# Retention attention and a top-2 mixture of experts: three more early pieces, from a fourth weight buffer laid over the attention output

## The chip, the cores and the metric

The kernel runs on one core of one Trainium2 chip. The metric is the device time of one execution in microseconds, the median of several runs. A profile of one further execution gives where each engine was busy or idle. The engines are called PE (matrix products), ACT, DVE and POOL (element-wise work; POOL also issues the indirect transfers) and SP (issues most of the other transfers).

## The reference

Attention with a decay over 8 batches, 8 heads, 576 positions and a head size of 64 gives 4608 tokens of 512 values. A router picks the two best of 8 experts for each token, and each expert is two products of 512 x 1024 and 1024 x 512 with a relu between them.

```
scores = q @ k^T / sqrt(64)
x      = (scores * Dmat) @ v                      # Dmat: gamma[h] ** (row - column), 0 above the diagonal
x      = x.transpose(0, 2, 1, 3).reshape(4608, 512)
noisy  = x @ w_gate + log1p(exp(x @ w_noise)) * noise
top2   = the two largest of noisy in each row; weights = softmax over these two
for e in 0..7:
    rows = tokens that have e among their two
    out[rows] += weight * (relu(x[rows] @ w1[e]) @ w2[e])
```

All inputs and the output are 32-bit floats in device memory. The weights of one expert are 4 MB.

## The kernel before, in words

**Attention and routing.** The 8 batches are worked in four pairs (`bp` 0 to 3). The attention output of a pair is kept turned in an `xT` buffer (two buffers, used in turn: 128 partitions x 4608 values of bf16 each). `route(bp)` computes the router for the pair from it, gives every (token, expert) choice a place in that expert's list, makes the table `xi{bp}` of which token stands at which place, turns the rows back (L1096) and stores them with their weights to `xd` in device memory (L1105, issued by SP).

**Pieces.** The list of an expert has 1216 places, cut in 9 pieces of 128 and one of 64. Choices where the expert is the lower-numbered of a token's two come first (`FIRST` says how many places they have). Places fill in the order of the tokens, so the first places of a list are known before the last pair is routed. `CLOSE` says, for each of the first three routings and each expert, up to which place the list is held to be closed after it. Pieces below that mark are run early; if too few tokens have come, the places up to the mark stay empty and later tokens go behind it.

**Early tiles.** `tiles()` makes early tiles of up to two pieces. `fetch` gathers their rows from `xd` (L1232, POOL), turns them on PE (L1254). `up` is the first product (L1314) with a relu on ACT (L1323) or DVE (L1325), `down` the second (L1404). `finish` scales the result by the token's weight (L1457 on ACT, L1459 on DVE) and scatters it to the output (L1469, POOL). Before the change there are 9 early tiles: 6 pieces of expert 0, 5 of expert 1, 4 of expert 2.

**Wide tiles.** After the last routing the other pieces run in tiles of up to four (512 columns). `wide` is their first product (L1340); the second product of the tile before is woven into it (L1404; L1423 for the piece of 64). Their rows are gathered up to three tiles ahead and turned by DMA (L1244, issued by SP), except those of expert 3, which PE turns (L1254). Gathers are spaced by `PACE`.

**Weights.** There are three weight buffers of 2 MB in bf16 (`W`). Experts 0 to 2 come early by converting transfers that POOL issues (L1145, L1149). The weights of a later expert come in 8 parts of 512 KB: SP loads a part as 32-bit floats into a buffer `big` (L1169, L1172; at most 4 `big` buffers for this), and ACT or DVE casts it into `W` (L445, L447). `weights(e + 3)` is called at the last tile of expert e, so expert 3 takes the buffer of expert 0, expert 4 that of expert 1, and so on. `SPREAD` says after how many steps (one step is one of the 8 column groups of a wide tile) the next part is due: 0 for expert 3, 3 for 4 and 5, 4 for 6 and 7.

**Order.** Every operation is recorded with a cost, its readers and writers and a priority. The planner `Plan.run` then sets the order on each engine before anything is issued: it simulates the engines and takes, again and again, the operation that can start earliest, and among equals the one of the smaller priority number. Buffers are granted in the order of recording within each class and use. Each engine, SP included, then works its list strictly in that order, and waits on the chip are those that the data and buffers need. A tile `i` has the priority 100 + 4 i. A table `ORDER` adds an offset for each kind of operation, by the range that the priority is in: the last two of its six columns are for 60 to below 136, and for 136 and above.

Of the kernel before, what the change touches and what calls it, by code (L numbers as in the profile page):

```python
# [10 lines left out]
BF16 = mybir.dt.bfloat16  # L11
I32 = mybir.dt.int32
# [5 lines left out]
P = 128  # L18
N = 4608
NCOL = N // P  # L20
E = 8
F = 1024
DM = 512
KD = DM // P
KF = F // P
HPE = 10
CAP = 1216
NH = E * HPE
# [2 lines left out]
SPREAD = (0, 0, 0, 0, 3, 3, 4, 4)  # L31
PACE = 2.343
AHEAD = (2, 3)
CLOSE = ((256, 0, 0, 0, 0, 0, 0, 0), (512, 384, 384, 0, 0, 0, 0, 0), (768, 640, 512, 0, 0, 0, 0, 0))
PLW = 8
XW = DM // 2 + PLW
ORDER = {
# [154 lines left out]
C9 = 9  # L192
# [211 lines left out]
class Kernel:  # L404
    def __init__(self, tc, ctx, src, gates, noise, w1, w2, out, xd):
        self.tc, self.nc = tc, tc.nc
        self.src, self.gates, self.noise, self.w1, self.w2, self.out = src, gates, noise, w1, w2, out
        self.xd = xd
        nc = self.nc
        self.pl = pl = Plan()  # L410
        self.cp = ctx.enter_context(tc.tile_pool(name="fix", bufs=1))
        self.ps = ctx.enter_context(tc.tile_pool(name="ps", bufs=1, space=bass.MemoryType.PSUM))
        mk = lambda n, k, sh, dt: [(self.cp.tile(sh, dt, name=f"{n}{i}"), None) for i in range(k)]
        bs = [self.cp.tile([P, 2, 1024], F32, name=f"big{i}") for i in range(5)]
        pl.cls("big", [(x[:, i, :], x) for x in bs for i in range(2)], exp=4, xt=3, rt=1)
        pl.cls("half", mk("half", 21, [P, 512], F32), cs=9, exp=15, xt=3, tl=6, rt=1)
        pl.cls("tb", mk("tb", 5, [P, 2, 4, P], BF16))
        pl.cls("xT", mk("xT", 2, [P, KD, C9, P], BF16))
        xs = [self.cp.tile([P, 2, XW], F32, name=f"xg{i}") for i in range(12)]
        pl.cls("xg", [(x[:, i, :], x) for x in xs for i in range(2)], exp=14, rt=10)  # L420
        pl.zone["xg", "exp"], pl.zone["xg", "rt"] = (10, 24), (0, 10)
        ws = [self.cp.tile([P, KD * F + KF * DM], BF16, name=f"W{i}") for i in range(3)]
        pl.cls("W", [(x, None) for x in ws])
        part = lambda x, i, n: x[:, 2 * i * n:2 * i * n + 2 * n].bitcast(F32)
        pl.cls("wkv", [(part(x, i, 2048), None) for x in ws[1:] for i in range(2)])
        pl.cls("wq", [(part(ws[0], i, 1024), None) for i in range(4)])
        pl.cls("ps", [(self.ps.tile([P, 512], F32, name=f"ps{i}"), None) for i in range(8)], exp=4, xt=2, rt=2, tl=2, rw=2, att=7)
        pl.cls("pay", mk("pl", 2, [P, 3], F32))
        self.fixed = {}
        pl.warm = self.warm  # L430
        self.xdk, self.outk = pl.fix(), {}
        self.writes, self.reads, self.firsts = [], [], {e: [] for e in range(E)}
# [493 lines left out]
    def route(self, bp, prio):  # L926
        pl, nc, f = self.pl, self.nc, self.fix
# [3 lines left out]
        xT = self.xT.pop(bp)  # L931
# [28 lines left out]
        m1, w2, rs, d2, x = (f(n, [P, C]) for n in ("max1", "wb", "rs", "d2", "low1"))  # L960
# [50 lines left out]
        pr = self.psum("rt")  # L1011
# [56 lines left out]
                                 start=(c == 0), stop=(c == 2 * C - 1), skip_group_check=True)  # L1068
        pl.op("PE", 1.3, table, r=[olo, oh], w=[(pT, 0)], prio=prio, late=0, at="route40")
        L = f("L", [P, NH])  # L1070
        xi = f(f"xi{bp}", [P, HPE * 3 if bp < 3 else NH], I32)
        nx = xi.t.shape[1]
        if bp == 0:
            o("DVE", 0.25, lambda e: V.tensor_copy(xi.t, pT.t[:, :nx]), [(pT, 0)], [xi], at="route41")
# [13 lines left out]
        for g in ((0, 2), (2, 2), (4, 2), (6, 2), (8, 1)):  # L1088
            c, n = g
            p, xr = self.psum("rw"), pl.buf("xg", "rt", 2)  # L1090

            def rows(e, c=c, n=n, p=p):
                o_ = p.t.bitcast(BF16).rearrange("p (c d) -> p c d", c=2)
                for k in range(n):
                    for di in range(KD):
                        nc.tensor.transpose(o_[:, k, di * P:(di + 1) * P], xT.t[:, di, c + k, :], ident.t)  # L1096
            b = c // 4
            rd = [(xT, (hq, b, e)) for hq in range(2) for e in range(2)] if b < 2 else [(xT, (2, 0)), (xT, (2, 1))]
            o("PE", 0.31 * n, rows, rd + [ident], [p], at="route47")
            o({"ACT": 0.17 + 0.43 * n, "DVE": 0.15 + 0.28 * n}, 0, lambda e, n=n, p=p, xr=xr: self.copy(  # L1100
                e, xr.t.bitcast(BF16)[:, :n, :DM], p.t.bitcast(BF16).rearrange("p (c d) -> p c d", c=2)[:, :n]), [p], [(xr, 0)], prio=prio + 1, at="route48")
            o({"POOL": 0.3, "DVE": 0.2}, 0, lambda e, c=c, n=n, xr=xr: self.eng(e).tensor_copy(
                xr.t[:, :n, DM // 2:], pay.t[:, c:c + n, :]), [pay], [(xr, 1)], at="route49")
            row = 1 + (c0 + c) * P
            pl.op("SP", 0.55, lambda e, n=n, xr=xr, row=row: nc.sync.dma_start(  # L1105
                out=self.xd[row:row + n * P, :].rearrange("(c p) w -> p c w", p=P), in_=xr.t[:, :n]),
                r=[xr], w=[(self.xdk, (bp // 2, bp, c))], prio=prio, dma=n * 0.4, at="route50")

# [27 lines left out]

    def weights(self, e, prio, cast_dma, after=()):
        pl, nc = self.pl, self.nc
        w = self.W[e] = pl.buf("W", "exp")
        if cast_dma:  # L1140
            for k in range(0, 8, 2):
                def go(_, k=k):
                    o = w.t[:, k * F:(k + 2) * F]
                    if k < KD:
                        nc.gpsimd.dma_start(out=o.rearrange("p (do f) -> p do f", do=2),  # L1145
                                            in_=self.w1[e, k * P:(k + 2) * P, :].rearrange("(do di) f -> di do f", di=P))
                    else:
                        fo = 2 * (k - KD)
                        nc.gpsimd.dma_start(out=o.rearrange("p (fo d) -> p fo d", fo=4),  # L1149
                                            in_=self.w2[e, fo * P:(fo + 4) * P, :].rearrange("(fo fi) d -> fi fo d", fi=P))  # L1150
                self.wdma.append(pl.op("POOL", 0.85, go, w=[(w, k), (w, k + 1)], prio=prio, dma=2.9,
                                       after=list(after) + self.wdma[-2:-1], at="weights1"))
            return
        for k in range(8):
            self.parts.append((self.step + SPREAD[e] * k, e, k))
        self.due(prio, after)
# [353 lines left out]
    def record(self):  # L1510
        pl = self.pl
# [9 lines left out]
        for u in range(NU + 1):  # L1521
            bp = u // 4
# [31 lines left out]
        for e, u in enumerate(WAIT):  # L1554
            raw = (("wkv", "att"), ("wq", "att"))[e == 0]
            self.weights(e, (40, 14.6, 14.7)[e], True, landed(u) + [o for b in pl.fifo[raw] for o in b.ops])

        fetched = 0
        for i, t in enumerate(ts[:ne]):
# [12 lines left out]
        for i in range(ne, len(ts) + 1):  # L1572
# [4 lines left out]
            if i < len(ts):  # L1577
# [5 lines left out]
                            self.before(i, ts[i], s, pr - 4)  # L1583
                if i == last[E - 2]:
                    self.before(i, ts[i], [self.size(j) for j in ts[i][1]].index(CAP % P), pr)
                if i == last[e] and e + 3 < E:
                    self.weights(e + 3, pr, False, begun)
                begun = [self.wide(i, ts[i], pr, prev)]
            else:
                e, po, hT = ts[-1][0], self.t[i - 1]["po"], self.t[i - 1]["hT"]  # L1590
# [141 lines left out]
```

## Time and profile before

| | |
|---|---|
| timed runs | 414.92, 413.98, 415.88 us; median 414.92 |
| span of the profiled execution, first to last instruction | 423.6 us (no other time of that execution is given) |
| PE busy | 379.1 us (89%) |
| POOL, ACT, DVE busy | 277.5, 271.2, 147.8 us |
| data moved by DMA | 98.06 MB, 231 GB/s over the span |
| last routing's table is built (L1067) | 161.5 to 162.4 us |
| first wide tile begins (L1340) | 191.2 us |
| expert 3's weight loads are issued | 188.5 to 208.7 us |

The span is cut below into stretches by these points: attention with routing and early tiles, early tiles alone, wide tiles. In rows of a timeline the first number is the start in us from the beginning of the span, the second the duration, and in brackets stands how long the engine was idle before it and what ended that. "issue" means that the profile shows nothing the engine waited for.

### The profile page before, as it was taken

What the parts mean: (1) busy time and instruction counts of PE and PEld (TensorE: products, weight loads), DVE (VectorE), ACT (ScalarE), POOL (GpSimd) and SP (SyncE); (2) the same over time, 40 slices, a digit from 0 to 9 for tenths busy, and PEclk for the clock granted to TensorE, in tenths of its full rate; (3) what the DMA queues carried; (4) which work ended last, traced back from release to release, by engine and by line L of the source; (5) the groups of instructions that cost most, each with busy time, mean ns of one, the idle gap of its engine ahead of it and who ended that gap; (6) DMA issues with size and microseconds to landing.
All of it is one profiled execution on the core that took longest, in us unless ns stands there. A gap on an engine that the chain in (4) does not pass through costs nothing.

```text
span 423.6 us, 10900 instructions
## 1 busy us (share of the span) xinstructions
PE 379.1 (89%) x4252; PEld 233.2 (55%) x4286; DVE 147.8 (35%) x415; ACT 271.2 (64%) x466; POOL 277.5 (66%) x345
## 2 busy tenths in 40 slices
PE   6898869777998997879999999999999896999993
PEld 2567657666676775645565544544544442454452
DVE  7357797896498595000313220200010000000002
ACT  3489978896887763545675796576676371655550
POOL 8577766872799465555476766777656672628554
PEclk9899998999999999999999999999999997999999
DMA  8999999999989994669899999999999999959775
GB/s 227 290 305 272 320 300 295 289 248 256 322 200 236 248 254 150 142 174 307 240 279 367 271 234 272 277 219 274 235 213 146 266 164 223 196 79 128 128 92 123
DMA packets 106184, 98.06 MB, mean 231 GB/s; under 512 B 40975, under 2 KB 83472, under 8 KB 106130
## 3 DMA queue, kind: packets, MB, share of 16 engines
q1 hardware_dynamic: 85858, 60.92, 56.2%
q0 software_dynamic: 17584, 36.24, 42.6%
q8 instruction: 34, 0.56, 0.6%
q10 hardware_dynamic: 2688, 0.18, 0.4%
q14 instruction: 20, 0.16, 0.1%
HBM read 73.11 MB, written 26.10 MB: 234 GB/s over the span
## 4 chain that ended last, share of the span: by engine, by line
PE 49%; DMA 20%; issue 9%; DVE 9%; POOL 6%; ACT 4%; ACTq 0%; POOLq 0%; SPq 0%; another core or an unknown queue 0%; DVEq 0%
PE ps L1404 17%; PE ps L1340 14%; DMA xg<-xd,xi 7%; PE ps L1314 6%; POOL out_dram L1469 5%; DMA big<-xg 3%; DMA out_dram<-half,im 3%; DMA out_dram<-half,xg 2%; DMA W<-in_moe_w_dram 2%; PE ps L794 2%; DVE half L769 2%; PE ps L829 2%; ACT half L445 1%; DMA W<-in_q_dram 1%; PE ps L453 1%
## 5 line engine op out<-in xcount | busy, mean ns | idle before, releaser
L1404 PE MATMUL ps<-W,half 128*128 128x512 bf16 x543 | 181.0, 382 | 6.2 <-ACT half L1323 4.7
L1340 PE MATMUL ps<-big,W 128*128 128x512 bf16 (+4 forms) x631 | 179.7, 331 | 6.6 <-issue 4.6
L1323 ACT ACTIVATE half<-ps 128x512 bf16<-128x512 f32 (+5 forms) x181 | 89.0, 508 | 73.3 <-PE ps L1340 47.5
L1232 POOL DMA_INDIRECT xg<-xd,xi x76 | 78.3, 1031 | 68.1 <-issue 18.3
L1469 POOL DMA_INDIRECT out_dram<-half,xg x71 | 90.7, 1278 | 33.0 <-issue 13.9
L1340 PEld LDWEIGHTS <-W 128*128 128x128 bf16 x640 | 62.9, 98 | 54.7 <-issue 8.5
L1404 PEld LDWEIGHTS <-half 128*128 128x128 bf16 x568 | 55.0, 98 | 68.5 <-ACT half L1323 7.0
L445 ACT ACTIVATE W<-big 128x1024 bf16<-128x1024 f32 x37 | 38.7, 1059 | 19.8 <-DMA big<-in_moe_w_dram 19.8
L1457 ACT ACTIVATE half<-ps,xg 128x512 f32<-128x512 f32 (+1 forms) x61 | 41.4, 679 | 13.1 <-PE ps L1404 12.0
L445 ACT ACTIVATE half<-ps 128x1024 bf16<-128x1024 bf16 (+1 forms) x40 | 37.6, 962 | 12.2 <-remote 3.6
L769 DVE TENSOR_TENSOR half<-ps,mask 128x512 bf16<-128x512 f32 x64 | 40.0, 682 | 14.1 <-PE ps L761 10.7
L1325 DVE TENSOR_SCALAR half<-ps 128x192 bf16<-128x192 f32 (+3 forms) x15 | 7.5, 500 | 78.0 <-PE ps L1340 19.8
L1314 PE MATMUL ps<-half,W 128*128 128x256 bf16 (+1 forms) x288 | 30.3, 255 | 1.9 <-issue 1.7
L1314 PEld LDWEIGHTS <-W 128*128 128x128 bf16 x288 | 23.7, 98 | 5.9 <-issue 2.3
L1455 DVE SCALAR_TENSOR_TENSOR half<-ps,xg,half 64x256 f32<-64x256 f32 (+2 forms) x7 | 3.6, 521 | 62.3 <-PE ps L1423 39.5
L445 ACT ACTIVATE tb<-ps 64x512 bf16<-64x512 f32 x32 | 18.9, 590 | 8.5 <-PE ps L794 6.2
L453 PE MATMUL ps<-mask,ident__61 128*128 128x512 bf16 x66 | 20.2, 439 | 3.7 <-DVE hpf L513 3.7
L1459 DVE TENSOR_SCALAR half<-ps,xg 64x256 f32<-64x256 f32 (+1 forms) x14 | 8.3, 596 | 42.9 <-PE ps L1423 21.0
L445 ACT ACTIVATE xT<-ps 128x512 bf16<-128x512 f32 (+1 forms) x32 | 16.2, 552 | 3.1 <-PE ps L879 1.8
L794 PE MATMUL ps<-half,half 64*64 64x64 bf16 (+2 forms) x512 | 16.8, 210 | 1.6 <-issue 0.9
L445 ACT ACTIVATE xg<-ps 128x1024 bf16<-128x1024 bf16 (+1 forms) x19 | 17.0, 939 | 1.8 <-PE ps L1096 1.1
L761 PE MATMUL ps<-half,half 64*64 64x128 bf16 x512 | 11.7, 218 | 7.1 <-ACT half L445 4.1
(196 smaller groups left out, 434.8 us busy)
## 6 DMA issues: line engine op xcount, KB each, us to landing
big<-in_moe_w_dram SPq DMA_DIRECT2D x40, 512.0 KB
W<-in_moe_w_dram POOLq DMA_DIRECT2D x12, 512.0 KB
xd<-xg SPq DMA_DIRECT2D x16, 264.0 KB
W<-in_q_dram SPq DMA_DIRECT2D x16, 256.0 KB
big<-in_k_dram SPq DMA_DIRECT2D x8, 512.0 KB
big<-in_v_dram SPq DMA_DIRECT2D x8, 512.0 KB
big<-in_q_dram SPq DMA_DIRECT2D x16, 256.0 KB
W<-in_k_dram SPq DMA_DIRECT2D x6, 512.0 KB
```

The costliest lines, as they stand in the source:

```text
L445: self.nc.scalar.activation(out, in_, Act.Copy)
L453: self.nc.tensor.matmul(b.t, lhsT=ident, rhs=mask.rearrange("p r x -> p (r x)").unsqueeze(1).to_broadcast([P, 2, 2 * P]), start=True, stop ...
L761: nc.tensor.matmul(o[h][e * HD:(e + 1) * HD, c, r], lhsT=kt[s, hp, c, r, e, :], rhs=qt[s, hp, :, 16 * j:16 * j + 16], start=(c == 0 and r ...
L769: nc.vector.tensor_tensor(S.t.bitcast(BF16).rearrange("p (h c x) -> p h c x", h=2, c=2)[:, h], p[h].t.rearrange("p (c x) -> p c x", c=2), ...
L794: nc.tensor.matmul(o[h * HD:(h + 1) * HD, hp, n, :], lhsT=kk[:k, r, c, y], rhs=vv[:k, r, c, y].unsqueeze(1).to_broadcast([k, n.stop - n.st ...
L1232: ins = nc.gpsimd.indirect_dma_start(out=x.t[:n, :], out_offset=None, in_=self.xd[:rows, :], in_offset=IOff(ap=xi.t[:n, h:h + 1], axis=0), ...
L1314: nc.tensor.matmul(pv()[:, f2, :], lhsT=w.t[:, o:o + P], rhs=xv()[:, di, :n], start=(di == 0), stop=(di == KD - 1))
L1323: self.nc.scalar.activation(o, i, Act.Relu)
L1340: self.mm = nc.tensor.matmul(p.t[:, :n], lhsT=w.t[:, o:o + P], rhs=xv()[:, di, :n], start=(di == 0), stop=(di == KD - 1))
L1404: self.mm = self.nc.tensor.matmul(po.t, lhsT=hv[:, c:c + P], rhs=self.W[e].t[:, o:o + DM], start=(f == 0), stop=(f == KF - 1))
L1457: nc.scalar.activation(y.t[q, c], x, Act.Copy, scale=g()[q])
L1469: ins = nc.gpsimd.indirect_dma_start(out=self.out[:, :], out_offset=IOff(ap=ix()[q2], axis=0), in_=y.t[q2, :], in_offset=None, bounds_chec ...
```

## The change

`CLOSE` gets 384 for expert 3 after the third routing, so pieces 0 to 2 of expert 3 become two early tiles (two pieces, and one) behind the nine; its wide pieces are now 7, in tiles of 4 and 3. Their priorities are 136 and 140, and all wide tiles' numbers rise by 8. The table `xi2` is widened from 30 to 40 columns to hold expert 3.

The two `xT` buffers become halves of one tile, and a fourth weight buffer `W4` (8192 of the 9216 values of a partition) is laid over them. Expert 3's weights go there: its 8 parts are recorded with priority 60, and the planner holds them until all work on the `xT` buffers is done and the last store to `xd` has landed. Each later expert's weights are called for at the last tile of the expert four before it instead of three: expert 4 takes the buffer of expert 0, 5 that of 1, 6 that of 2, and expert 7 takes `W4` after expert 3. `SPREAD`, `ORDER`, `PACE` and `FIRST` are as they were.

```diff
-CLOSE = ((256, 0, 0, 0, 0, 0, 0, 0), (512, 384, 384, 0, 0, 0, 0, 0), (768, 640, 512, 0, 0, 0, 0, 0))
+CLOSE = ((256, 0, 0, 0, 0, 0, 0, 0), (512, 384, 384, 0, 0, 0, 0, 0), (768, 640, 512, 384, 0, 0, 0, 0))
...
-        pl.cls("xT", mk("xT", 2, [P, KD, C9, P], BF16))
+        xts = self.cp.tile([P, 2, KD * C9 * P], BF16, name="xT")
+        pl.cls("xT", [(xts[:, i].rearrange("p (k c s) -> p k c s", k=KD, c=C9), None) for i in range(2)])
+        pl.cls("W4", [(xts.rearrange("p b x -> p (b x)")[:, :KD * F + KF * DM], None)])
...
-        xi = f(f"xi{bp}", [P, HPE * 3 if bp < 3 else NH], I32)
+        xi = f(f"xi{bp}", [P, (HPE * 3, HPE * 3, HPE * 4, NH)[bp]], I32)
...
-            pl.op("SP", 0.55, lambda e, n=n, xr=xr, row=row: nc.sync.dma_start(
+            self.stored = pl.op("SP", 0.55, lambda e, n=n, xr=xr, row=row: nc.sync.dma_start(
...
-        w = self.W[e] = pl.buf("W", "exp")
+        w = self.W[e] = pl.buf("W4" if e % 4 == 3 else "W", "exp")
...
+        w = self.W[3] = pl.buf("W4", "exp")
+        for k in range(8):
+            self.part(3, k, 60, [o for b in pl.fifo["xT", "att"] for o in b.ops] + [self.stored])
...
-                if i == last[e] and e + 3 < E:
-                    self.weights(e + 3, pr, False, begun)
+                if i == last[e] and e + 4 < E:
+                    self.weights(e + 4, pr, False, begun)
```

## The prediction

> **What bounds the kernel now.** I read the page first, then a table of six stretches of the span.
>
> ```profile
> span 423.6 us, 10900 instructions
> PE 379.1 (89%) x4252; PEld 233.2 (55%) x4286; DVE 147.8 (35%) x415; ACT 271.2 (64%) x466; POOL 277.5 (66%) x345
> big<-in_moe_w_dram SPq DMA_DIRECT2D x40, 512.0 KB
> ```
> ```profile
> core 0: us, PE busy (x) PEld busy (x) DVE busy (x) ACT busy (x) POOL busy (x), PEclk, DMA share, GB/s
> 0.00:162.20 162.20, 138.23 (x2812) 104.42 (x2820) 119.83 (x345) 122.19 (x205) 115.13 (x207) 0.98 1.05 270
> 162.20:191.20 29.00, 22.80 (x197) 15.31 (x198) 2.82 (x8) 12.34 (x23) 16.25 (x17) 1.00 0.60 146
> 191.20:330.00 138.80, 137.52 (x802) 72.26 (x816) 20.21 (x52) 94.34 (x157) 92.57 (x83) 1.00 1.08 254
> 330.00:361.00 31.00, 24.66 (x127) 11.87 (x128) 1.33 (x3) 12.88 (x25) 18.30 (x14) 0.89 1.21 225
> 361.00:410.00 49.00, 48.74 (x266) 24.61 (x270) 0.96 (x2) 27.27 (x52) 29.16 (x21) 1.00 0.81 125
> ```
>
> TensorE is the bound, most strictly after 191.2 us: 137.5 of 138.8 us and 48.7 of 49.0. Up to 162.2 it is attention and routing, where it loses 24 us; the change has no weights there yet, so that loss is out of its reach. Two places are left. From the end of the last routing's table (162.2) to the first wide tile (191.2) PE is idle for 29.0 - 22.8 = 6.2 us, with the DMA engines at 0.60. From 330 to 361 it is idle for 6.3 us, at a clock of 0.89 and with the DMA engines at 1.21.
>
> The timeline of PE shows the first place:
>
> ```profile
> 163.88 0.22 PE L1314 MATMUL ps<-half,W 128*128 128x128 bf16 x1 [0.36 <-issue]
> 165.34 1.11 PE L1314 MATMUL ps<-half,W 128*128 128x128 bf16 x17 [0.50 <-issue]
> 174.66 2.82 PE L1404 MATMUL ps<-W,half 128*128 128x512 bf16 x11 [1.26 <-ACT half L1323]
> 177.54 3.66 PE L1314 MATMUL ps<-half,W 128*128 128x256 bf16 x32
> 181.04 1.46 PE L1404 MATMUL ps<-W,half 128*128 128x512 bf16 x5
> 184.08 2.33 PE L1404 MATMUL ps<-W,half 128*128 128x512 bf16 x10 [1.59 <-ACT half L1323]
> 186.25 1.95 PE L1314 MATMUL ps<-half,W 128*128 128x128 bf16 x32
> 189.97 0.61 PE L1404 MATMUL ps<-W,half 128*128 128x512 bf16 x2 [0.90 <-ACT half L1323]
> 190.99 0.38 PE L1404 MATMUL ps<-W,half 128*128 128x512 bf16 x1 [0.42 <-ACT half L1323]
> 191.21 6.38 PE L1340 MATMUL ps<-big,W 128*128 128x448 bf16 x33
> ```
>
> PE is not short of data here. Early tiles fill it to the end, one after the other (first product on L1314, second on L1404). The second product stops in the middle until ACT has applied the last relu (L1323): 1.26, 1.59, then 0.90 + 0.42 us. The wide tile at 191.21 follows without a wait, so it was ready earlier.
>
> The chain of work that ended last, and PE's own rows, show the second place:
>
> ```profile
> 317.21 13.16 DMA xg<-xd,xi
> 330.48 6.19 DMA xg<-xd,xi
> 336.67 14.22 DMA big<-xg
> 350.89 4.02 issue
> 360.18 0.43 PE ps L1340
> 361.32 0.22 PE ps L1340
> ```
> ```profile
> 339.72 0.24 PE L1340 MATMUL ps<-big,W 128*128 128x192 bf16 x1 [1.32 <-ACT half L1323]
> 354.91 0.58 PE L1340 MATMUL ps<-big,W 128*128 128x512 bf16 x1 [4.21 <-issue]
> ```
> ```profile
> 335.22 1.06 ACT L445 ACTIVATE W<-big 128x1024 bf16<-128x1024 f32 x1 [5.20 <-DMA big<-in_moe_w_dram]
> ```
>
> A gather in flight for 13 us, one for 6, and a transposing DMA for 14 led to a PE stop of 4.21 us. After it matmuls came every 0.43 us instead of 0.22 until about 360.6, which costs (360.6 - 354.9) x (1 - 0.22/0.43) = 2.8 us. Ahead of it a weight cast held ACT for 5.20 us waiting on its load; the relus behind it cost PE 6.3 - 4.2 = 2.1 us. Together 9.1 us.
>
> **The change, part by part.**
>
> Work moved. Three 128-row pieces of expert 3 leave the wide tiles (512, 512, 192 columns become 512, 320) for two early tiles of 256 and 128 columns. Early price: 3.66 (32 matmuls of 256) + 1.95 (32 of 128) + 24 second products. Ten of those took 2.33 us, which is nine steps and one length of 0.38, so 0.217 each and 5.2 in all: 10.8 us. Wide price: 32 x 0.217 x 384/512 = 5.2, and again 5.2: 10.4. Net +0.4 us on PE. Expert 3's pieces are turned on PE in both versions. So there is no gain on PE but where the moved work stands in a gap that exists.
>
> Gaps. Each early tile of the timeline ends in its own wait: 1.59 for a 256-column tile, 0.90 + 0.42 for a 128-column one, so two tiles add up to 2.9 us. At the other end expert 3's matmuls could stand in the four waits of the rows: -4.2. The order is the planner's: earliest start, then the smaller priority number. Expert 3's early tiles have 136 and 140, behind all other early tiles, and the rows show no matmul of a later tile in an earlier tile's wait. That is nearest to the upper end; the wide tile may stand in some of it. I take +1.5.
>
> The weights. The queue of SP and the last reads of the attention output:
>
> ```profile
> 156.92 0.95 SPq L1105 DMA_DIRECT2D xd<-xg  x2
> 170.01 18.48 SPq L1244 DMA_TRANSPOSE big<-xg  x9
> 188.54 2.44 SPq L1169 DMA_DIRECT2D big<-in_moe_w_dram  x4
> 204.79 3.93 SPq L1172 DMA_DIRECT2D big<-in_moe_w_dram  x4
> ...
> 210.20 10.34 SPq L1169 DMA_DIRECT2D big<-in_moe_w_dram  x4
> 221.54 9.47 SPq L1172 DMA_DIRECT2D big<-in_moe_w_dram  x4
> ...
> 341.45 2.99 SPq L1172 DMA_DIRECT2D big<-in_moe_w_dram  x2
> ```
> ```profile
> L1096 PE MATMUL ps<-ident__61,xT x36: 216/219/229, 137.6 to 145.1; 128*128 128x128 bf16 x36
> ```
> ```profile
> 166.76 1.03 POOL L1232 DMA_INDIRECT xg<-xd,xi  x1 [2.51 <-DVE xi L1083]
> ```
>
> The output's buffers are last read at 145 and the last store to xd is issued by 157.9, so laying the fourth buffer over them costs nothing. Expert 3's eight loads (4.2 MB), today at 188.5 to 208.7, move to just behind 157.9. The stretch moves 146 GB/s where the one before it moved 270. With all of that rate the loads land by 157.9 + 4.2/0.27 = 173.5; with only the difference (124 GB/s) by 192. Expert 3's first product is due behind the present early work, at 191.2, and its second some 4 us later; until then that early work is the cover. So no wait (0), or about 1 us if the slow end holds and the last cast is late. I take 0. If that early work were gone, the wait would be the whole load.
>
> Their eight casts on ACT cost 1.06 us each, 8.5 us, beside 12.3 busy of 29.0: they fit. But ACT works in order, and a relu behind a cast whose load is late waits with it: 2.1 us in the rows of 335 to 340. Bounds 0 and 2.1; DMA is at 0.60 here against 1.21 there, so +0.5.
>
> SP. The loads go ahead of the first transposing DMA (170.01, itself waiting on a gather issued at 166.76). Eight loads issue in about 4 us when unblocked, and SP is free from 157.9 to 170.0. Should a load wait for its staging buffer, the transposes behind it wait too; the first wide tile is now due some 12 us later, and that covers it. POOL gets three gathers and three scatters of about 1.03 us earlier, 6 us beside 16.3 busy of 29.0, and as many fewer later: 0. Its gathers for the first wide tile may slip by 3 us, under the same cover. The wider table (40 for 30 columns) and the wrapper of the store: nothing.
>
> Late phase. Every later expert's weights start one expert earlier (4 behind expert 0 instead of 1, up to 7 behind expert 3 instead of 4, in the buffer that expert 3 gives up). Today the last loads are issued at 341 to 344, just ahead of the stop at 351. A wide piece costs 8 + 8 steps of 0.217 us, 3.47 us. With the wide tiles from about 203 on, experts 0 to 2 (13.5 pieces) end near 250, expert 2's last tile begins at 241 and expert 3's last at 250 + 4 x 3.47 = 264. Expert 7's loads begin there and are spread over 28 of the steps of which a tile has 8, some 40 us: they end near 305 to 310, with only gathers, transposes and scatters afterwards. That removes between 0 and 9.1 us. In the profiled execution I take 6 of it. Against the median it is less: the three timed runs are 8.7 us shorter than the profiled span (414.92 against 423.6, no other time being given for that execution), nearly as much as these stops cost, so much of them may belong to tracing. That is nearer to 0 and I take -2.5.
>
> The Trainium skill's TensorE: Matmul & The Clock Gate, The HAM clock gate, says that the clock is halved after an idle window of about 3.4 us and restored after about as long at work; the 0.43 for 0.22 us behind the 4.21 us stop agrees. By that rule a stop shortened below its window would return 2.8 us more than its own length, which makes this term rather all or nothing than a quarter.
>
> Sum: +0.4 + 1.5 + 0 + 0.5 - 2.5 = -0.1 us, so 414.8 against the median of 414.9. For the profiled execution: 423.6 + 2.4 - 6 = 420.
>
> **The rivals.**
>
> Faster: the stops at 337 to 355 are also in the timed runs, and go. Half to all of 9.1 us: 414.9 + 2.4 - (4.6 to 9.1) = 408.2 to 412.7. For it speaks that the chain runs through DMA from 317 to 351; against it that the timed runs are shorter by as much. If expert 3's matmuls fill the four early waits as well, it is 4.2 + 1.5 us lower still, which I think unlikely.
>
> Slower: crowding. Expert 6's weights now start at about 241 and expert 7's at about 264, each spread over some 40 us, where today they start at the last tiles of experts 3 and 4, a whole expert (33 us) apart. So two sets of loads share the DMA engines between about 264 and 281, in a stretch whose share is already 1.08. A cast that waits 5 us there stops PE as at 335, or a transpose comes late as at 351, and the stop moves forward instead of going: 414.9 + 2.4 + (0 to 7.0) = 417.3 to 424. It decides as soon as a gather or transpose there is in flight longer than the three tiles of lead it has. Against it: 16 loads were issued between 188.5 and 231 today, with no PE stop worth naming.
>
> Slower: expert 3's weights come late for its early tiles, because loads, stores and gathers share engines. At the slow end above the last load lands at 192 and later with queueing; with a 4 us stop and the slow clock behind it, 414.9 + 2.4 + 4 + 2.8 = 424. The Trainium skill's DMA: Bandwidth & Descriptors, Issuing engines are not separate DMA queues, says that transfers of SP and POOL interleave on the same 16 engines; no row here shows more than the shares, and the 30 us of cover stand against it.
>
> No effect as meant: the early pieces are run, but in place of wide work of equal price, and the late relief is nothing in untraced runs: 414.9 + 2.4 = 417.3, at the edge of slower.
>
> **How the numbers follow.** Half a per cent, 2.1 us, is about what a measurement of this kernel can tell from no change: 412.8 to 417.0 is the same. My forecast, early cost and late relief cancelling within that: 0.37. Faster (408.2 to 412.7): 0.32. Slower: 0.31, of which crowding 0.13, late weights 0.06, no relief 0.12. The likeliest one's own range is 412.8 to 417.0. The range of 8 in 10 leaves out the ends of both sides, about 0.1 each: 409.5 to 420.5.
>
> **What would show it.** Right: the early stretch ends near 203 instead of 191 with two more relu waits and no PE wait on loads or casts of W; loads of weights begin near 158 and end near 310; between 330 and 361 PE is over 0.95 busy at full clock. Wrong: a PE wait on a cast before 205; an ACT wait of several us on a load between 160 and 190; a PE stop between 262 and 310; the first wide tile at or before 197, which would mean that the gaps were filled; or the stop near 351 still there.

## The result, and the profile after

The changed kernel took 432.39 us in the median of four runs (425.46 to 439.56), the kernel before 415.12 (413.98 to 415.88). The ratio is 1.0264, with a 95% interval of 1.0202 to 1.0326: slower, and above the range that was forecast. The ratio leaves disturbed executions out, here and below, which is why it need not be that of the medians. The profiled execution of the changed kernel took 425.46 us at a span of 423.9. By the same 1.5 us the profiled execution of the kernel before, whose span was 423.6, took about 425 and was 10 us longer than its timed runs, so two spans that look alike stand for kernels 10 us apart.

From line 419 on all lines of the changed kernel are two higher: the first product of an early tile is L1316, the second L1406, the wide tiles L1342, the table L1069. The same five stretches of its span, cut at its own table and its own first wide tile:

```profile
core 0: us, PE busy (x) PEld busy (x) DVE busy (x) ACT busy (x) POOL busy (x), PEclk, DMA share, GB/s
0.00:165.00 165.00, 138.58 (x2819) 104.06 (x2820) 118.95 (x345) 122.40 (x205) 115.07 (x207) 0.98 1.03 266
165.00:210.20 45.20, 37.15 (x296) 24.16 (x293) 6.55 (x15) 21.91 (x36) 22.02 (x22) 0.89 0.72 223
210.20:330.00 119.80, 118.35 (x703) 61.94 (x702) 19.13 (x48) 78.78 (x138) 81.36 (x72) 1.00 1.04 260
330.00:361.00 31.00, 31.00 (x176) 15.72 (x175) 0.97 (x2) 17.45 (x33) 23.21 (x20) 1.00 0.97 181
361.00:410.00 49.00, 49.00 (x269) 24.52 (x268) 0.96 (x2) 25.74 (x49) 29.35 (x22) 1.00 0.75 113
```

The late stops are gone (31.00 of 31.00 busy). The loss is in the second row: PE is idle for 8 us and has a clock of 0.89 there, instead of 6.2 us and 1.00. PE's timeline just behind the table, start and length first, the idle time ahead in brackets:

```profile
164.34 0.81 PE L1069 MATMUL ps<-oh,olo 128*128 128x80 f16 x18 [0.29 <-issue]
164.98 0.61 PE L1256 MATMUL ps<-ident__61,xg 128*128 128x128 bf16 x8
165.43 0.89 PE L1316 MATMUL ps<-half,W 128*128 128x128 bf16 x13
167.33 0.22 PE L1316 MATMUL ps<-half,W 128*128 128x128 bf16 x1 [1.01 <-issue]
168.05 0.28 PE L1316 MATMUL ps<-half,W 128*128 128x128 bf16 x2 [0.50 <-issue]
169.46 0.58 PE L1316 MATMUL ps<-half,W 128*128 128x128 bf16 x4 [1.14 <-issue]
170.90 0.58 PE L1316 MATMUL ps<-half,W 128*128 128x128 bf16 x4 [0.86 <-issue]
172.32 0.37 PE L1316 MATMUL ps<-half,W 128*128 128x128 bf16 x2 [0.84 <-issue]
173.05 1.02 PE L1316 MATMUL ps<-half,W 128*128 128x128 bf16 x6 [0.36 <-issue]
```

The 32 matmuls of this early tile, which can follow each other at 0.06 us, take from 165.4 to 174.1: thirteen, and from there on one to six and a pause each time. I call this the hold; its last pause ends at 173.05. The engines that read PE's results see it too; DVE and ACT:

```profile
171.02 0.24 DVE L1080 TENSOR_SCALAR Ls<-ps 128x80 f32<-128x80 f32 x1 [5.10 <-remote]
173.84 1.02 ACT L447 ACTIVATE half<-ps 128x1024 bf16<-128x1024 bf16 x1 [9.05 <-remote]
```

DVE got the table at 171.0, six microseconds after it ended at 165.15; ACT got the transposes of 165.6 at 173.8. Then the clock gives way; one window, its clock being the third number from the right:

```profile
170.00:180.00 10.00, 7.21 (x34) 3.90 (x34) 2.18 (x6) 2.13 (x5) 1.99 (x2) 0.52 0.98 371
```

The kernel before has the same hold, shorter, with the last pause ending at 165.34. The rows at 163.88 and 165.34 that the prediction quotes are part of it, and here is its table reaching DVE, 3.2 us after it ended:

```profile
165.50 0.24 DVE L1078 TENSOR_SCALAR Ls<-ps 128x80 f32<-128x80 f32 x1 [2.41 <-remote]
```

What stood beside it was POOL. Around the last routing's table the kernel before issues six indirect transfers 0.3 us apart, from a scatter at 156.68 to one at 163.25. Its next gather needs the new table (`xi`), the one that is late, so POOL then waits until 166.76:

```profile
161.94 1.00 POOL L1469 DMA_INDIRECT out_dram<-half,xg  x1 [0.30 <-issue]
163.25 1.00 POOL L1469 DMA_INDIRECT out_dram<-half,xg  x1 [0.30 <-issue]
166.76 1.03 POOL L1232 DMA_INDIRECT xg<-xd,xi  x1 [2.51 <-DVE xi L1083]
```

The changed kernel goes straight on with expert 3's three gathers, which use an older table:

```profile
164.78 1.01 POOL L1471 DMA_INDIRECT out_dram<-half,xg  x1 [0.30 <-issue]
166.09 0.99 POOL L1471 DMA_INDIRECT out_dram<-half,xg  x1 [0.30 <-issue]
167.38 1.05 POOL L1234 DMA_INDIRECT xg<-xd,xi  x1 [0.30 <-issue]
168.73 1.02 POOL L1234 DMA_INDIRECT xg<-xd,xi  x1 [0.30 <-issue]
170.06 1.00 POOL L1234 DMA_INDIRECT xg<-xd,xi  x1 [0.31 <-issue]
172.28 0.99 POOL L1234 DMA_INDIRECT xg<-xd,xi  x1 [1.23 <-issue]
```

### The profile page after: what moved, and what is told of

Read it like the earlier page. It is cut to its first block, busy times and chain, and to the rows that moved or that the text cites. A ratio compares the mean times of both kernels' runs of the same rounds, so it can differ in the third digit from the quotient of the medians.

```text
span 423.9 us, 11007 instructions
## 1 busy us (share of the span) xinstructions
PE 382.3 (90%) x4318; PEld 235.7 (56%) x4318; DVE 149.2 (35%) x416; ACT 269.1 (63%) x466; POOL 277.9 (66%) x345
## 4 chain that ended last, share of the span: by engine, by line
PE 56%; DMA 12%; DVE 8%; issue 7%; POOL 6%; ACT 5%; another core or an unknown queue 3%; SPq 1%; ACTq 0%; POOLq 0%; DVEq 0%
PE ps L1406 23%; PE ps L1342 19%; PE ps L1316 6%; POOL out_dram L1471 4%; DMA xd<-xg 3%; DMA big<-in_moe_w_dram 3%; DMA noise<-in_moe_noise_dram 3%; DVE half L771 2%; DMA big<-in_v_dram 2%; ACT half L447 2%; DMA big<-in_k_dram 2%; PE ps L1425 1%; ACT half L1325 1%; DVE olo L1062 1%
## 5 line engine op out<-in xcount | busy, mean ns | idle before, releaser
L1406 PE MATMUL ps<-W,half 128*128 128x512 bf16 x432 | 139.3, 383 | 4.3 <-ACT half L1325 3.5
L1342 PE MATMUL ps<-big,W 128*128 128x512 bf16 (+4 forms) x448 | 124.0, 326 | 0.0
L1406 PEld LDWEIGHTS <-half 128*128 128x128 bf16 x568 | 54.8, 98 | 67.7 <-ACT half L1325 6.5
L1342 PEld LDWEIGHTS <-W 128*128 128x128 bf16 x448 | 43.8, 98 | 34.1 <-issue 1.7
L1342 PE MATMUL ps<-big,xT 128*128 128x512 bf16 (+2 forms) x160 | 47.6, 337 | 0.0
L1406 PE MATMUL ps<-xT,half 128*128 128x512 bf16 x136 | 45.0, 379 | 0.3 <-issue 0.2
L1461 DVE TENSOR_SCALAR half<-ps,xg 128x512 f32<-128x512 f32 (+1 forms) x18 | 11.4, 632 | 81.0 <-PE ps L1425 48.8
L1316 PE MATMUL ps<-half,W 128*128 128x256 bf16 (+1 forms) x288 | 33.3, 267 | 7.0 <-issue 4.7
L1316 PEld LDWEIGHTS <-W 128*128 128x128 bf16 x288 | 25.2, 102 | 12.5 <-issue 8.0
L447 ACT ACTIVATE W<-big 128x1024 bf16<-128x1024 f32 x22 | 23.4, 1068 | 8.7 <-DMA big<-in_moe_w_dram 7.7
L1342 PEld LDWEIGHTS <-xT 128*128 128x128 bf16 x160 | 15.7, 98 | 12.8 <-issue 0.4
L1327 DVE TENSOR_SCALAR half<-ps 128x512 bf16<-128x512 f32 (+4 forms) x9 | 4.8, 528 | 49.6 <-PE ps L1342 27.2
```

The source lines that it names most:

```text
L447: self.nc.scalar.activation(out, in_, Act.Copy)
L1316: nc.tensor.matmul(pv()[:, f2, :], lhsT=w.t[:, o:o + P], rhs=xv()[:, di, :n], start=(di == 0), stop=(di == KD - 1))
L1327: self.nc.vector.tensor_relu(o, i)
L1342: self.mm = nc.tensor.matmul(p.t[:, :n], lhsT=w.t[:, o:o + P], rhs=xv()[:, di, :n], start=(di == 0), stop=(di == KD - 1))
L1406: self.mm = self.nc.tensor.matmul(po.t, lhsT=hv[:, c:c + P], rhs=self.W[e].t[:, o:o + DM], start=(f == 0), stop=(f == KF - 1))
L1461: nc.vector.tensor_scalar(y.t[q, c], x, g()[q], None, Alu.mult)
```

## The experiments

Five theories were tried. A: the burst of eight weight loads, now in this stretch, holds PE. B, called D from e5 on: the added tiles and their order cost the time. C: POOL's unbroken run of transfers holds PE, and the three gathers make the hold longer. P, beside C: what holds PE is that POOL is busy, with whatever. F, added later: whether there is a hold at all depends on something outside the kernel. Runs that were made beside each other, with the kernel before among them, are called a group: e1 to e4, e5 to e8, e9 to e11, e12 to e14, e15, e16, and e17 with e18. The recorded expectations call the hold a crawl.

**e1, the loads alone.** The kernel before, with eight more loads behind the last store to xd:

```
+ for k in range(8):
+     t = pl.buf("big", "exp")
+     pl.op("SP", 0.05, load of w2[3] into t, w=[t], prio=60, after=[self.stored])
```

> The kernel before, with eight extra loads of 512 KB issued back to back by SP right behind the last store to xd, where the changed kernel has expert 3's loads. Nothing reads them, and nothing else is moved: the orders on PE, DVE and POOL are those of before. Theory A (the burst itself: eight loads in flight at once hold up PE right after the last routing's table): the PE gaps marked issue that come after the table grow from some 1.4 us to 6 to 8 us with the clock down behind them, the first wide tile starts 8 to 10 us later, and the time is 420 to 426 us. Theory B (the two added early tiles and the order that comes with them cost the time; the loads are hidden): the first wide tile stays within 2 us of where it was and the time is 415 to 417 us.

Measured: 420.3 us in the median (414.49 to 427.66), the kernel before beside it 418.07, ratio 0.997 (0.9891 to 1.0049). The hold is that of the kernel before: PE has only two pauses, and DVE waits 2.28 us for the table (2.41 in the kernel before). Theory A falls.

**e2, the pieces without their weights.** The same early tiles in the kernel before, but with expert 2's weights, so that nothing is loaded early; the results of these three pieces are not expert 3's.

```
- CLOSE = (..., (768, 640, 512, 0, 0, 0, 0, 0))
+ CLOSE = (..., (768, 640, 512, 384, 0, 0, 0, 0))
+ self.W[3] = self.W[2]          # early tiles only
```

> Expert 3's three early pieces as in the changed kernel, but multiplied with expert 2's weights, which are already there; expert 3's own weights come late, in three buffers, as before (so the values of these pieces are not expert 3's). Theory A: no stop behind the table beyond that of before; the first wide tile is some 11 to 14 us later than before and the three pieces are missing from the wide phase, so the time is 414 to 418 us. Theory B: two more relu waits and the shifted order cost as much as in the changed kernel, 424 us or more.

Measured: 437.4 us, ratio 1.044 (1.0343 to 1.0537). The hold is there in full though no weights are loaded (DMA share 0.14 between 170 and 180): eight pauses, the last one ending at 172.14, and the first wide tile at 209.40. Part of its time lies later (PE is idle for 13.3 us in the wide phase), so the place is worth more here than the ratio.

**e3, the weights without the pieces.** The changed kernel with expert 3's entry in CLOSE back at 0.

> The changed kernel without the early pieces: expert 3's weights still go to the fourth buffer by the eight loads behind the last store, later experts' weights come one expert earlier, but all ten pieces of expert 3 are wide. Theory A: the stop behind the table is there as in the changed kernel, the first wide tile starts 8 to 10 us later than before with no work moved out of the wide phase, and the time is 421 to 427 us. Theory B: 414 to 417 us.

Measured: 414.94 us, ratio 0.9939 (0.9888 to 0.999). The hold is short again:

```profile
164.42 0.27 PE L1316 MATMUL ps<-half,W 128*128 128x128 bf16 x2 [0.29 <-issue]
165.84 1.11 PE L1316 MATMUL ps<-half,W 128*128 128x128 bf16 x17 [1.15 <-issue]
190.89 1.30 PE L1342 MATMUL ps<-big,W 128*128 128x448 bf16 x6
```

**e4, the loads slowed.** The changed kernel with expert 3's loads through two staging buffers instead of the common ones.

> The changed kernel with expert 3's parts loaded through two staging buffers only, so that a load waits for the cast two before it and no more than 1 MB is in flight. Theory A: the stop behind the table shrinks towards that of before (1 to 3 us), and the time falls to 415 to 420 us, if the waits of SP on casts do not cost as much elsewhere. Theory B: no better than the changed kernel, 425 us or more.

Measured: 427.12 us, ratio 1.0224 (1.0151 to 1.0297); last pause until 171.95, first wide tile at 210.44. With e1 to e4 the early pieces had brought the loss; weights, loads and the buffer laid over the attention output had not. What of the pieces was open: their tiles or their gathers.

**e5, the gathers alone.** The kernel before, with three gathers into buffers that nobody reads behind the scatter of 163.25.

```
+ self.nsc += 1
+ if self.nsc == 9:              # behind the ninth scatter
+     for k in range(3):
+         nc.gpsimd.indirect_dma_start(out=dum[k], in_=xd viewed in rows of 176, in_offset=column of xi2)
```

> The kernel before, with three extra gathers on POOL (128 rows of 176 elements, into buffers that nobody reads) right behind the scatter that ends at 164.3 in its trace, where the changed kernel has expert 3's three; the order on PE, DVE, ACT and SP is the same instruction for instruction. Theory C (POOL's indirect transfers, issued back to back behind the last routing, hold up PE's completions): the crawl of the single-column early tile lasts from about 163 to 169-172 instead of 165.4, the granted clock falls below 0.8 in 170-180, the first wide matmul comes at 196-201 instead of 191.2, and the time is 421 to 426. Theory D (the order or the added tiles on PE cost the time, the gathers don't): first wide matmul 191-193, time 414 to 417.

**e6, POOL busy without transfers.** The same place, 18 fills instead.

> The kernel before, with 18 fills of 128x176 on POOL (some 2 to 4 us of POOL time, no transfer) at the same place as the three extra gathers. It leaves nothing out. Theory C: no hold, since no transfer is issued; first wide matmul 191-194, time 414 to 417. Rival P (POOL being busy is what holds up PE or the copies, whatever it does): crawl until 168 or later, time 419 or more.

**e7, the gathers elsewhere.** The three gathers ahead of the fifth scatter.

> The kernel before, with the same three extra gathers but issued at about 143 to 147, ahead of the scatter at 151.4, where POOL is idle and issues nothing else back to back. Theory C: the place decides, so nothing changes: first wide matmul 191-193, time 414 to 417. A rival (any three more gathers cost PE some 2 us each, wherever they are): 419 to 423.

**e8, the pieces with their gathers held back.** The changed kernel; each of expert 3's early gathers waits for the last matmul recorded ahead of it, those of the first product included. The order on all engines stays.

```
- if pace:
+ if pace or (early, e) == (2, 3):
      self.tc.add_manual_dep(ins.ins, self.mm.ins.name, ...)
```

> The changed kernel, in which each of expert 3's three early gathers waits for the last matmul recorded ahead of it on PE; the order on every engine is that of the changed kernel. Theory C: the run of indirect transfers behind the last routing ends with the two scatters as in the kernel before, the crawl ends near 168-169 instead of 174, the granted clock stays above 0.9 in 170-180, the first wide matmul comes at 200-204 instead of 210.2, and the time is 413 to 418. Theory D: the crawl and 425 to 430 stay.

Measured in this group: the kernel before 409.74 us in the median of 25 runs; e5 413.96, ratio 1.0063 (0.9991 to 1.0136); e6 421.44 without a usable ratio; e7 417.06, ratio 1.0123 (1.0049 to 1.0197); e8 408.72, ratio 0.9971 (0.9909 to 1.0033). None of the four profiles shows a hold. So neither P, nor the gathers by themselves (e5), nor their place (e7) were put to the test with a hold; no run here does that. e5, with its transfers as tight as in the changed kernel:

```profile
164.05 1.01 POOL L1469 DMA_INDIRECT out_dram<-half,xg  x1 [0.30 <-issue]
165.36 1.04 POOL L1496 DMA_INDIRECT dum<-xd,xi  x1 [0.30 <-issue]
166.71 1.02 POOL L1496 DMA_INDIRECT dum<-xd,xi  x1 [0.31 <-issue]
168.04 1.01 POOL L1496 DMA_INDIRECT dum<-xd,xi  x1 [0.30 <-issue]
```
```profile
163.43 1.95 PE L1314 MATMUL ps<-half,W 128*128 128x128 bf16 x32
185.01 6.38 PE L1340 MATMUL ps<-big,W 128*128 128x448 bf16 x33
```

The same 32 matmuls run through in 1.95 us beside them. So theory C as it stood falls: transfers alone do not make a hold. And the kernel before was itself 5 to 8 us faster than in the comparisons ahead (415.12 and 418.07). Hence theory F, and the changed kernel once more:

**e9, e10, e11: the changed kernel, e8 and e5 again, in one group.**

> The changed kernel once more, beside the next two on one chip. In the call before this one no kernel showed the crawl behind the last routing, not even the one with three extra gathers, while all six profiles taken ahead of it did. Theory C (POOL's transfers hold PE): where the paced kernel of the same call is free of the crawl, this one has it, first wide matmul near 210, ratio 1.02 to 1.03. Theory F (the crawl comes with the chip, and the order of POOL's transfers only sets how long it lasts): on a chip where the kernel before has no crawl, this one has none either, first wide matmul 193 to 196, ratio 0.99 to 1.00.

> The changed kernel with expert 3's three early gathers waiting for PE, as before. Theory C: 1.5 to 3% faster than the changed kernel of this call, by a crawl that is 5 us shorter and a clock that is not halved. Theory F on a chip without the crawl: the same time as the changed kernel, ratio to the kernel before 0.99 to 1.00; on a chip with it: as theory C.

> The kernel before with the three extra gathers behind the last routing. Theory C, and F on a chip with the crawl: crawl to 169-172, first wide matmul 196 to 201, ratio 1.01 to 1.03. F on a chip without it: no crawl, first wide matmul 185 to 188, ratio 0.995 to 1.01.

Measured: again no hold. The kernel before 409.52 us, the changed one 412.58 in the median of four (407.99, 408.04, 417.13, 417.83; the kernel before from 406.61 to 423.47), without a usable ratio. The lowest times of the two, elsewhere 10 to 11 us apart, were 1.4 us apart here. The changed kernel's timeline at the same place:

```profile
161.90 0.81 PE L1069 MATMUL ps<-oh,olo 128*128 128x80 f16 x18 [0.29 <-DVE oh L1064]
162.99 1.95 PE L1316 MATMUL ps<-half,W 128*128 128x128 bf16 x32
195.34 0.92 PE L1342 MATMUL ps<-big,W 128*128 128x448 bf16 x4
```

e10 took 418.01 us (408.19 to 421.68) without a usable ratio, e11 417.48 with 1.0185 (1.0071 to 1.0299), above the 0.995 to 1.01 that I expected. e11 has no hold and its first wide tile at 185.03, so that its loss, and the smaller one of e7, lies elsewhere; where, I did not find. Nor is a hold a matter of full DMA engines: in e9 their share is 0.99 between 162 and 167, without a hold, and in the kernel before 0.41 between 160 and 170, with one.

**e12, e13, e14: the changed kernel, the paced one and the one without pieces, with more executions.**

> The changed kernel, in five rounds. On chips where the kernel before shows no crawl behind the last routing (its time is 406 to 411) theory F says no crawl here either: first wide matmul 195, ratio 0.990 to 1.000. On a chip with the crawl (the kernel before at 415 to 418): first wide matmul 207 to 210, ratio 1.02 to 1.03. A theory by which the added early tiles themselves cost the time says 1.02 or more on both.

> The changed kernel with expert 3's three early gathers waiting for PE, in five rounds. On a chip without the crawl: as the changed kernel within 0.5%. On a chip with it, theory C (POOL's unbroken run of transfers keeps the crawl going): the crawl ends near 168-169, 414 to 418, ratio 0.995 to 1.005; if the crawl has nothing to do with POOL's transfers: 425 or more, as the changed kernel.

> The changed kernel without the three early pieces (weights in the fourth buffer, their loads behind the last routing), in five rounds. On either kind of chip PE's early work is that of the kernel before: first wide matmul 185 (without the crawl) or 191 (with it), ratio 0.99 to 1.00; if the changed kernel is faster than this one where there is no crawl, the moved pieces are worth something by themselves, and I expect at most 0.3% of that.

Measured, without a hold: the kernel before 410.93 us; e12 413.75, ratio 1.0005 (0.9933 to 1.0077); e13 418.56 without a usable ratio; e14 412.12, ratio 1.0094 (1.0042 to 1.0146). The changed kernel's change of 2.6% is gone. My expectation of e14 was wrong: without the pieces the early weights cost about 0.9%. PE runs out of early work, waits for the transposed rows of the first wide tile, and works on at a clock of 0.63 (22 matmuls in 6.74 us):

```profile
189.56 6.74 PE L1342 MATMUL ps<-big,W 128*128 128x448 bf16 x22 [4.41 <-DMA big<-xg]
```
```profile
159.41 3.29 SPq L1174 DMA_DIRECT2D big<-in_moe_w_dram  x4
169.65 20.65 SPq L1246 DMA_TRANSPOSE big<-xg  x9
```

The loads stand ahead of the transposes in SP's queue, but that is not what delays them: the loads are issued by 162.70, and SP waits from there on for the gathers. The DMA engines are fuller: their share is 0.95 to 1.03 between 160 and 175, against 0.35 to 0.75 between 162.5 and 177.5 in e11, where the loads come later, and nine transposes take SP 20.65 us instead of 15.41 (e5). That the loads in flight slow the gathers and transposes is likely from this, but not shown by a run of its own. In e3 the hold had kept PE busy with early work until 190.9, which hid this.

**e15 and e16: the paced kernel again, in search of the hold.**

> The changed kernel with the paced gathers, once more, for a chip of the kind of the first comparison. Where the kernel before takes 415 to 418 (the crawl is there): theory C says that the crawl ends near 168-169 and the first wide matmul comes at 200-204, ratio 0.995 to 1.005; if POOL's transfers have nothing to do with it, the crawl lasts to 173 and the ratio is 1.02 or more. Where the kernel before takes 406 to 411 (no crawl): first wide matmul 194 to 196, ratio 0.99 to 1.00, which tells nothing new.

> The changed kernel with the paced gathers, another try for a chip with the crawl. Kernel before at 415 to 418: theory C says crawl until 168-169, first wide matmul 200-204; without a link to POOL's transfers, crawl until 173 and first wide matmul 207-210. Kernel before at 406 to 411: first wide matmul 194 to 196.

e15 met no hold: 413.79 us beside 411.19, ratio 0.9948 (0.9879 to 1.0016), first wide tile at 193.25. e16 met it (the kernel before at 418.97): the last pause ended at 166.13, 3.8 us after the table's start as in the kernel before, and the first wide tile came at 200.72, as theory C had said. The time did not follow: 426.15 us in two runs, ratio 1.0191 (1.0051 to 1.033). In the profiled one PE is idle for 12.8 us in the wide phase, 6.2 of them in one wait for a transpose at 325.77; whether that belongs to the pacing is open.

**e17 and e18: the changed kernel and the paced one beside each other.**

> The changed kernel beside the paced one. On a chip with the crawl (kernel before at 415 to 418): crawl to 172-174, first wide matmul 207 to 210, ratio 1.02 to 1.03. On one without: first wide matmul 195, ratio 0.99 to 1.005.

> The paced kernel beside the changed one. On a chip with the crawl: crawl to 166-169 and first wide matmul 200 to 204 as in the run before, 6 to 9 us ahead of the changed kernel; if this carries to the end, ratio 1.00 to 1.01; if the late stops of the wide phase seen in that run belong to the paced order, 1.02. On a chip without: ratio 0.99 to 1.005.

This group had the hold, on a chip that the records give the same number as in e12 to e15, which had none. So it does not go with that number; what it goes with, the runs do not show. The kernel before took 418.73 us, e17 434.46 (424.34 to 441.91), ratio 1.0301 (1.02 to 1.0402); e18 423.85 (420.12 to 429.27), ratio 1.0158 (1.0092 to 1.0225). Pacing gives back about half of the loss, the two intervals just overlapping. PE and POOL of e18:

```profile
167.33 0.22 PE L1316 MATMUL ps<-half,W 128*128 128x128 bf16 x1 [0.50 <-issue]
168.07 1.23 PE L1316 MATMUL ps<-half,W 128*128 128x128 bf16 x19 [0.52 <-issue]
182.44 0.27 PE L1316 MATMUL ps<-half,W 128*128 128x256 bf16 x1 [0.22 <-issue]
183.18 0.38 PE L1316 MATMUL ps<-half,W 128*128 128x256 bf16 x2 [0.47 <-issue]
184.62 0.35 PE L1316 MATMUL ps<-half,W 128*128 128x256 bf16 x1 [0.46 <-issue]
```
```profile
165.97 0.99 POOL L1471 DMA_INDIRECT out_dram<-half,xg  x1 [0.30 <-issue]
169.12 1.04 POOL L1234 DMA_INDIRECT xg<-xd,xi  x1 [2.16 <-PE ps L1316]
179.44 1.00 POOL L1234 DMA_INDIRECT xg<-xd,xi  x1 [0.30 <-issue]
182.53 0.99 POOL L1471 DMA_INDIRECT out_dram<-half,xg  x1 [0.78 <-issue]
185.77 1.04 POOL L1234 DMA_INDIRECT xg<-xd,xi  x1 [2.25 <-issue]
```

With POOL pausing from 167.0 to 169.1 the last pause of the first hold ends at 168.07, 3.8 us after the table's start; in e17 it took 8.1 us. But the transfers that were put off now follow each other from 171.4 to 183.5, and a second hold stands from 182 to 185, with the clock at 0.73 between 180 and 190. Thus, where the hold exists, its length goes with how long POOL works on without a pause, shown by holding three gathers back (e18 beside e17; e16 agrees). Where it doesn't exist, the same transfers do nothing (e5, e9, e11, e12). Whether transfers are needed, or any work of POOL would do (P), stays open. Against P speaks only that the table starts at much the same time with the hold (161.5 to 164.3) and without (159.8 to 164.6), although POOL is busy for 115 of the 165 us up to it, some 80 of them without a transfer (profile of the changed kernel).

From the table's start to the first wide tile, all in one view, worked out from these two rows of each kernel's timeline (e8, e10 and e13 are 0.5 to 1 us above e15; e14 has the wait for transposes in it):

| PE's early work | with the hold | without |
|---|---|---|
| that of the kernel before | before 29.7, e1 30.2, e3 28.7 | e5 22.7, e6 22.7, e7 23.3, e11 22.7, e14 29.8 |
| with expert 3's pieces | after 45.8, e2 46.7, e4 47.1, e17 44.7 | e9 33.4, e12 35.0 |
| with pieces, gathers paced | e16 38.4, e18 41.5 | e15 32.5 |

No version of these beats the kernel before on both sides of the table: e3 is 0.994 with the hold and, as e14, 1.009 without it; e8 and e15, the paced kernel without the hold, have intervals that include 1.

## Why the prediction was wrong

**Moved work, +0.4: right.** Without the hold the stretch grows by 33.4 - 22.7 = 10.7 us (10.8 was worked out), and PE's busy time in the wide phase falls from 215.85 us (e3) to 205.60 (e9), 10.3 against 10.4.

**Gaps, +1.5 with bounds of -4.2 and +2.9: the step that failed.** I read the stops of 1.26, 1.59 and 0.90 + 0.42 us in the second products as the price that an early tile has by itself, and priced two more tiles by them. They came with the hold: without it the order of the kernel before loses at most 0.2 us in that stretch (e5, e6, e11), not 6.2, and two more tiles add a wait of 0.75 us on a gather (e9) or one of 2.1 us behind a cast (e12, see below). With the hold the stretch grew by 16.1 us (45.8 - 29.7), of which 10.8 are work: the gaps cost 5.3 against this profile of before, 6.3 against e3 (45.8 - 28.7 - 10.8). Only 1.9 of the 5.3 us are more idle time of PE (8.06 us against 6.20 from the table's start to the first wide tile), close to the 1.5 by luck; the other 3.4 are matmuls at the lower clock behind the hold, for which the term had nothing. The two pauses at 163.88 and 165.34 were in my first quoted rows, named "issue", which means that nothing in the profile explains them, and I passed over them because ACT's waits were longer. The whole loss against e3, 10.5 us of span, is a stretch that is 17.1 us longer, a table that starts 2.2 us later and a wide phase that is only 8.7 us shorter where 10.3 us of work had left it; the last two I did not trace further.

**POOL, 0: the mis-read cover.** Three gathers of 1.03 us were set against POOL's idle time, 16.3 busy of 29.0. That counts room on POOL, where it does fit. What it does to PE is a matter of POOL's pause between 164.25 and 166.76, in which the hold ended. The three gathers need no new table, so they filled just that. The row that showed the pause, the gather at 166.76 with [2.51 <-DVE xi L1083], was quoted for something else.

**Weights, 0: right; casts, +0.5: within its bounds.** In the changed kernel's profile no matmul waits on a load or cast of W before 205. The loads were issued from 160.72 to 320.19, where 158 to 310 was forecast; issuing the first eight took 5.3 us, not about 4.

```profile
160.72 2.70 SPq L1171 DMA_DIRECT2D big<-in_moe_w_dram  x4
163.46 2.55 SPq L1174 DMA_DIRECT2D big<-in_moe_w_dram  x4
...
320.19 1.07 SPq L1174 DMA_DIRECT2D big<-in_moe_w_dram  x2
```

A relu did wait behind a cast whose load was late, as the term says, but only without the hold: not in e9, and for the upper bound of 2.1 us in e12.

```profile
183.74 1.06 ACT L447 ACTIVATE xT<-big 128x1024 bf16<-128x1024 f32 x1 [2.43 <-DMA big<-in_moe_w_dram]
```
```profile
185.35 1.67 PE L1406 MATMUL ps<-W,half 128*128 128x512 bf16 x7 [2.10 <-ACT half L1325]
```

That the first wide tile's late date covers a delay of its transposes was right: with the cover gone (e14) PE waits 4.41 us. The reason given, a load that waits for its staging buffer, was not the one.

**Late relief, -2.5 (-6 in the profiled execution): half right.** The stops of 337 to 355 do not come back in the changed kernel, but they were hardly in the timed runs of before either, as far as one trace can tell: e1, with the wide phase of the kernel before and a profiled execution of 417.29 us, loses 1.1 us on PE in the whole of it (215.78 busy of 216.90). So there was next to nothing to relieve, and the term is about 0. "Nearer to 0" was right, the -2.5 was not.

**The rivals.** The slower ones named crowding and late weights; neither happened (PE is 47.51 of 48 us busy between 262 and 310, and e1 and e2 clear the loads). The third, no relief in untraced runs, was right in its condition but gives 417.3, far below what was measured. So slower came true for none of the reasons given; the cause stood in the sum as gaps of 1.5 us. Without the hold the forecast of no change holds (e12, 1.0005), with it the change costs 2.6 to 3.0%; that both kinds of execution exist could not be seen in one trace.

**The clock.** In the hold the longest pause is 1.14 us, and the clock still fell, to 0.85 in 168 to 170 and 0.50 in 170 to 172, with PE busy for 1.35 of the 4 us from 166 to 170. In the shorter holds of before, e1 and e3 it stayed at 1.00. So here a stretch that was mostly idle sufficed, without being idle throughout, and a stall of many small pauses has to be priced with the half clock behind it. The Trainium skill's TensorE: Matmul & The Clock Gate, The HAM clock gate, puts the half clock behind an idle window of about 3.4 us; no pause of the hold was that long.

## What to carry to other kernels

A pause named "issue" has no cause in the profile: before work is added to the stretch it stands in, look what the other engines do during it and where it ends, and price the added work as if the pause grows with it. Count the pauses of a queue, not only its free time; a transfer that fits into an idle gap of POOL removes the gap. And when two kernels are compared, see from the kernel before, run beside each of them, whether it ran the same way: the same edit was worth 0.05% or 3% by a condition that the kernel before shows in its own time (medians of 409.5 to 411.2, or of 415.1 to 419.0 us).

## What the runs showed of the hardware

PE can be held up where the profile shows nothing that it waits for. In the groups with the hold, 32 matmuls that otherwise take 1.95 us took 3.7 to 8.7 us, in bunches 0.7 us or a multiple of it apart (167.33, 168.05, 169.46, 170.90, 172.32, 173.05), and DVE and ACT waited 2.28 to 9.05 us for what PE had ended before. In the kernel before, e1, e3, e16 and e18 the last pause ended 0.9 to 1.1 us behind the end of POOL's run, whose last transfer was a scatter; in the changed kernel, e2, e4 and e17, where gathers end the run, 1.4 to 2.0 us behind. Gathers without a scatter ahead of them, at 166.76 to 170.4 in the kernel before, held nothing. Two of the stops that the prediction read as relu waits look the same: ACT, on which PE waited, sat idle until 174.01 and 183.43, 1.0 and 1.1 us behind the end of a scatter (172.03 + 1.01 and 181.31 + 1.00). In other groups the same instructions showed none of it. By what path POOL's work reaches PE, and what sets the two kinds of group apart, stays open.
